# Fetching the transposed activations two tiles at a time, and a new place in the load queue for strip two's keys, values and last queries

## The chip, the cores and the metric

The kernel runs on one core of one Trainium2 chip. The metric is the device time of one execution in microseconds (us); lower is better. The kernel before was timed at 876.93 us, the median of three runs (875.13 to 880.14 us).

## What is computed

An attention block without softmax feeds a feed-forward block with squared ReLU. All values are float32. The inputs `q`, `k`, `v` have 8 batches, 8 heads, 576 positions and 64 features per head.

```python
kv  = einsum('bhsd,bhse->bhde', k, v)            # 64 x 64 per head
out = einsum('bhsd,bhde->bhse', q, kv)
rms = sqrt(mean(out * out, axis=-1, keepdims=True) + 1e-6)
x   = (out / rms * g_norm)                       # then (B,H,S,D) -> (4608 tokens, 512)
h   = x @ w_in                                   # 512 -> 2048
y   = (maximum(h, 0) ** 2) @ w_out               # 2048 -> 512
```

## The kernel before

**Tiles and strips.** The 4608 tokens are 36 tiles of 128 tokens, and 4 tiles make a strip of 512 tokens, so there are 9 strips, numbered s = 0 to 8 in the code. The change calls s = 2 "strip two" and s = 3 "strip three". For each strip the feed-forward block runs an up phase (x times `w_in`) and a down phase (times `w_out`). Both are cut by Strassen-like recombinations into sums and differences of blocks, so a strip has fewer products on TensorE (PE) and more additions on VectorE (DVE), ScalarE (ACT) and GpSimd (POOL). From strip 2 on (`DEEP_UP = 2`) both phases are recombined twice: the up phase has 55 steps (`up_slot`, L1248), the down phase 14 (`down_deep`, L1109), numbered 55 to 68. Nearly every up step is one group of 16 matmuls.

**Attention for later strips.** The attention part of a coming strip is spread between the steps of the present one. A list `slices` holds its pieces in order; `attend_between` (L778) decides per step which of them run, by planned costs on DVE and ACT. The pieces that matter here are `transposed_query` (L378: DVE transposes a loaded q tile), `key_value` (L415: K^T V on PE), `query` (L505: products of q with K^T V), `squares_x` (L641: DVE transposes 32x32 squares of a finished x tile into `x_q`) and `send_x` (L652: writes `x_q` to a scratch tensor `x_d` in DRAM). Tiles 9 to 35 take this way through DRAM.

**Reading x back.** `fetch_x` (L657) reads a tile from `x_d` into the strip's `xT` buffer with four transfers, one for each block of 32 partitions. It calls `open_xt` (L624), which takes a buffer for `xT` from the stream pool when the first tile of a strip is fetched. `xT` is the right-hand side of the up phase of that strip.

**Weights.** `stream` (L933) takes the next weight block into a buffer of the stream pool: `w_in_deep` blocks (768 KB) for the up phase, then for each of the seven down products one block from `w_out` (L945, 768 KB) and one from `w_deep` (L951, 1 MB). The pool has 6 buffers, one or two of them held by `xT`; an allocation takes the buffer that was freed longest ago, and its transfer waits until the last reader of that buffer is done. In the up phase `stream` runs at steps 10, 17, 24, 31, 38, 45 and 52, and once at step 5. The block taken at step 31 holds the first `w_out` block of the down phase, the one at step 38 the first `w_deep` block; PE reads them at steps 49, 51 and 53 of the up phase already (L1270) and again in the first down step. The block of step 45 is read from step 57 on, the one of step 52 in step 58.

**One queue for all transfers.** SyncE (SP) issues nearly all transfers, in program order: weights, outputs (L960), `x_d` writes, `xT` fetches, keys and values (L132, with `k_rest` and `v_rest` at L162), queries (L123, in half tiles of two transfers) and `q_rest` (L176). A transfer that has to wait holds up all behind it.

**Which step a load goes to.** `clock` counts planned microseconds: 1.2 for an up step from strip 2 on, 2.2 for an up step of strip 1, 3.2 for a down step. After each step at most one of three queues is served (L1401 to L1411): first `keys_due` (a key load falls due 2 us after the `key_value` that frees its buffer), then `tiles_due` (an x fetch falls due 6 us after its `send_x`, with longer times for tiles 9, 10 and 11), and only if neither was served `drip`, which takes one half of a q tile or one part of `q_rest`. Drips keep a least distance of 4.5 us in an up phase (2.1 us in strip 1, 3.3 us in a down phase) and stop in `quiet` steps, in strip 2 and later from step 37 to step 57.

Of the kernel before, what the change touches and what calls it, by code (L numbers as in the profile page):

```python
# [10 lines left out]
FP32 = mybir.dt.float32  # L11
# [9 lines left out]
def kernel(  # L21
# [34 lines left out]
    nc = tc.nc  # L56
    P = 128
# [4 lines left out]
    NP = H // 2  # L62
# [6 lines left out]
    NT = 4  # L69
# [2 lines left out]
    N_STRIP = N_TILE // NT  # L72
    DEEP = 1
    DEEP_UP = 2
    SQ = 32
    Q_ON_PE = 2
    BEHIND = 1.6
# [10 lines left out]
    dram = ctx.enter_context(tc.tile_pool(name="dram", bufs=1, space=bass.MemoryType.DRAM))  # L88
# [101 lines left out]
    drips, rest_drips, keys_due, tiles_due = deque(), deque(), deque(), deque()  # L190
    clock, dripped = [0.0], [0.0]

    def due(queue):
        if queue and queue[0][0] <= clock[0]:
            _, f, a = queue.popleft()
            f(*a)
            return True
# [376 lines left out]
    first = {}  # L574
# [49 lines left out]
    def open_xt(s):  # L624
        if s not in xt:
            if s == 0:
                xt[s] = xt_pool.tile([P, STRIP // SQ, NP, SQ], FP32, name="xT", tag="xT")
            else:
                t = stream_pool.tile([P, 4, FQ // 2, P], FP32, name="xT", tag="w_blk")
                xt[s] = t.rearrange("p n f e -> p (n f e)").rearrange("p (a q t) -> p a q t", q=NP, t=SQ)  # L630
        return xt[s]
# [18 lines left out]
    squared, sent = {}, {}  # L650

    def send_x(n):  # L652
        d = sent[n] = dram.tile([P, 4, NP, SQ], FP32, name="x_d", tag="x_d", bufs=2 * NT)
        nc.sync.dma_start(out=d, in_=squared.pop(n))
        tiles_due.append((clock[0] + {9: 30, 10: 36, 11: 24}.get(n, 6), fetch_x, (n,)))

    def fetch_x(n):  # L657
        s, i = divmod(n, NT)
        x, d = open_xt(s), sent.pop(n)
        for f in range(4):  # L660
            nc.sync.dma_start(
                out=x[ts(f, SQ), ts(i, 4)].rearrange("d a q t -> d a (q t)"),
                in_=d[:, f].rearrange("(a d) q t -> d a (q t)", a=4),
            )

    xc = {}
# [442 lines left out]
    def down_deep(s, k, i):  # L1109
# [3 lines left out]
        if s == N_STRIP - 1 and k == 6 and i == 1:  # L1113
# [19 lines left out]
            return  # L1133
        if k == 0 and s >= DEEP_UP:
            if i == 0:
# [202 lines left out]
    for s in range(N_STRIP):  # L1338
        attend(ready[s])
        if s == DEEP_UP - 1:  # L1340
            while queried:
                attend(slice_at[0] + 1)
            psums.close()
            fpsum = ctx.enter_context(tc.tile_pool(name="fpsum", bufs=5, space=bass.MemoryType.PSUM, reuse_waits="tile"))
            apsum = ctx.enter_context(tc.tile_pool(name="apsum", bufs=1, space=bass.MemoryType.PSUM, reuse_waits="tile"))
        if s >= DEEP_UP:
            steps = [(0.5, up_slot, (s, slot)) for slot in range(55)]
        elif s == 0:
            steps = [(2, up_first, (g, fh, i)) for g in range(NG) for fh in range(2) for i in range(2)]
        else:  # L1350
            steps = [(1, up, (s, g, p)) for g in range(NG) for p in ORDER]
        n_up = len(steps)
        if s < DEEP:

            steps += [(2, down, (s, p, i)) for p in (ORDER if s else (1, 2, 5, 6, 7, 3, 4)) for i in range(2)]
        else:
            steps += [(2, down_deep, (s, k, i)) for k in range(7) for i in range(2)]
        goal, begun = ready.get(s + 1, len(slices)), slice_at[0]
        if s >= DEEP_UP:
            goal = max(goal, min(ready[DEEP_UP] + (len(slices) - ready[DEEP_UP]) * (s - 1) // (N_STRIP - DEEP_UP - 1), len(slices)))  # L1360
            if s > DEEP_UP:
                goal = min(pair_ends, key=lambda end: abs(end - goal))
        total, done = sum(w for w, _, _ in steps), 0
        for i, (w, fn, a) in enumerate(steps):
            if s == 0 and i < n_up:

                if 4 <= i < 10:
                    convert(3 + i)
                if i == 0:
                    load_next()  # L1370
                    load_rest(1, nc.sync)
                    load_next()
                if i == 1:
                    load_next()
                if i == 2:
                    for b in range(2):
                        load_q_rest(b, nc.sync)
                if i == 14:
                    for b in range(2):
                        store_first(b)  # L1380
            elif s == 0 and i == n_up:
                convert(len(conversions))
                conv.close()

                stream_pool = ctx.enter_context(tc.tile_pool(name="stream", bufs=6, reuse_waits="tile"))
                sum_pool = ctx.enter_context(tc.tile_pool(name="sum", bufs=8, reuse_waits="tile"))
            if s == 0 and n_up <= i < n_up + 2:
                for g in range(2 * (i - n_up), 2 * (i - n_up) + 2):
                    sum_g1(0, g)
            if s == 0 and n_up + 2 <= i < n_up + 4:  # L1390
                for g in range(2 * (i - n_up) - 4, 2 * (i - n_up) - 2):
                    sum_g3(0, g)
            fn(*a)
            if s == 0 and i < 4:

                convert(3 + i)
            done += w
            if s:
                clock[0] += 3.2 if i >= n_up else 2.2 if s == DEEP else 1.2
                soon = tiles_due and tiles_due[0][2][0] // NT == s + 1  # L1400
                if i == n_up + 10:  # L1401
                    while tiles_due and tiles_due[0][2][0] // NT == s + 1:
                        _, f, a = tiles_due.popleft()
                        f(*a)
                elif not due(keys_due) and not (soon and due(tiles_due)):
                    least = 2.1 if s == DEEP else 4.5 if i < n_up else 3.3
                    quiet = n_up * 2 // 3 < i < n_up + 3 or s == DEEP and i > n_up + 9
                    quiet = quiet or s == DEEP and i < n_up and drips and drips[0][0] == load_q_rest
                    if not quiet and clock[0] >= dripped[0] + least:
                        dripped[0] = clock[0]  # L1410
                        drip(True)  # L1411
                if s == DEEP:
                    attend(begun + (goal - begun) * min(i + 1, 25) // 25)
                elif i < n_up:
                    attend_between(i, begun, goal, *(2, 34) if s == DEEP_UP else (0, 27), 38)
                if s == DEEP and i in (3, 4, 7, 9):
                    if i == 3:
                        last_sums = store_deep_sums(*deep_due.popleft())
                    next(last_sums, None)
                if s == DEEP and i == n_up - 3:  # L1420
                    leaf_sums(s, 4)
                if s == 1 and i in range(2, 23, 3):
                    deep_sums_in((1, 6, 5, 4, 0, 2, 3)[i // 3])
                if s == 1 and i in (17, 20, 21, 23):
                    stream()
                continue
            if i == n_up:
                nc.gpsimd.memset(open_xt(1)[:, 0, 0, 0:1], 0.0)
                stream(2)
            if i == n_up + 4:  # L1430
                stream()
            if i in (n_up + 8, n_up + 11):
                load(2, (i - n_up) // 11, nc.sync, "q")
            if i == n_up + 12:
                load_q_rest(2, nc.sync)
            if i - n_up in (7, 8, 9, 12):
                sums_in((7, 8, 9, 12).index(i - n_up))
            if i == n_up + 11:
                sums_x(1)
            n = i + 1 - (n_up - 6)  # L1440
            pairs, m = divmod(max(n - 2 * NP, 0), 3)
            attend(min(ready[0] + min(max(n, 0), 2 * NP) + (n >= 2 * NP) + 4 * pairs + (0, 2, 2)[m], goal))
            while deep_due and i not in (n_up + 1, n_up + 4, n_up + 12, n_up + 13):
                deque(store_deep_sums(*deep_due.popleft()), 0)
            if i == n_up + 2:
                store_first(2)
            if i == n_up + 3:
                for _ in range(2):
                    load_next(names="kv")
            if i == n_up + 6:  # L1450
                load_rest(2, nc.sync)
            if 11 <= i < n_up:

                convert((13, 13, 14, 15, 16)[i - 11])
# [30 lines left out]
```

## Time and profile before

| | before |
|---|---|
| time, median of 3 runs | 876.93 us (875.13 to 880.14) |
| the profiled execution | 876.18 us |
| its span, first to last instruction | 874.4 us |
| PE busy | 860.8 us (98%) |
| DVE busy | 722.9 us (83%) |
| ACT busy, POOL busy | 352.0 us (40%), 315.4 us (36%) |
| granted TensorE clock, mean | 1.000 |
| transfers on SP's queue | 82.5% of the 16 DMA engines' span, 234.33 MB |
| `xT` fetches | 108 of 64 KB |
| `x_d` writes | 27 of 256 KB |

The profile is of one execution. "Busy" is the time in which an engine works on an instruction; waiting for a semaphore and issuing a transfer do not count. The views that are used below: the page (shares, the chain of work that ended last, groups, DMA issues), the waits (who waited for whom: total us, times, longest), the timeline of one engine (start, duration, what, and in square brackets the idle time before it with what ended it) and the windows (busy time per engine in a stretch, granted clock, DMA share, GB/s). `SPq` is the queue of SP.

### The profile page before, as it was taken

The page shows a single profiled execution, that of the slowest core. Times are in us where ns is not written, and L with a number is a line of the kernel's source. Part 1 is how long each engine was busy: PE and PEld are TensorE (multiplying, and loading weights), DVE is VectorE, ACT ScalarE, POOL GpSimd, SP SyncE. Part 2 cuts the span into 40 slices and gives each one's busy share as a digit, 9 for nine tenths or more (in the row PEclk, how much of TensorE's full clock was granted, in tenths as well). Part 3 has the DMA queues.
Part 4 walks back from the last instruction along what each step waited for, and adds up shares of the span by engine and source line. Part 5 has one row for each costly group of instructions (what it writes and reads, how often), then busy time and mean ns, then how long its engine had stood idle before and what let it go on. Part 6 is the DMA issues. An engine that isn't in the chain of part 4 may idle for free.

```text
span 874.4 us, 32665 instructions
## 1 busy us (share of the span) xinstructions
PE 860.8 (98%) x14176; PEld 805.8 (92%) x14176; DVE 722.9 (83%) x1236; ACT 352.0 (40%) x805; POOL 315.4 (36%) x319
## 2 busy tenths in 40 slices
PE   8999999999999899999999999999999999999998
PEld 7445888889999899999999999999999999999998
DVE  3899998879867896889778977897889777975897
ACT  5799241320047402560358034811392147202710
POOL 1100004630458305650475045704471447144700
PEclk9999999999999999999999999999999999999999
DMA  9998998999988997989778978998668856885483
GB/s 306 328 311 251 285 372 237 283 339 346 305 219 205 338 328 242 239 290 338 245 213 261 344 268 228 271 346 287 189 238 293 295 173 218 299 283 196 175 313 120
DMA packets 170304, 236.49 MB, mean 270 GB/s; under 512 B 79536, under 2 KB 134576, under 8 KB 161840
## 3 DMA queue, kind: packets, MB, share of 16 engines
q1 hardware_dynamic: 169856, 234.33, 82.5%
q8 instruction: 111, 1.82, 0.8%
q14 instruction: 33, 0.27, 0.1%
q10 hardware_dynamic: 304, 0.07, 0.0%
HBM read 197.66 MB, written 36.70 MB: 268 GB/s over the span
## 4 chain that ended last, share of the span: by engine, by line
PE 82%; DVE 9%; DMA 4%; ACT 3%; issue 2%; SPq 1%; DVEq 0%; ACTq 0%
PE ps_A L842 35%; PE ps_B L842 30%; PE ps_C L842 5%; PE ps_A L847 4%; PE x_ps L468 2%; PE kv_ps L432 2%; PE ps_B L847 2%; DVE w_c L269 1%; DVE w_t L289 1%; DMA q<-in_q_dram 1%; DMA w_blk<-w_deep 1%; DMA w_deep<-w_t 1%; DVE wt L289 1%; DMA q_rest<-in_q_dram 1%; PE ps_C L847 1%
## 5 line engine op out<-in xcount | busy, mean ns | idle before, releaser
L842 PE MATMUL ps_B<-w_blk,g_s 128*64 128x128 f32 x2016 | 122.6, 273 | 0.0
L842 PEld LDWEIGHTS ps_B<-w_blk,g_s 128*64 128x64 f32 x2016 | 113.1, 137 | 0.1
L842 PE MATMUL ps_A<-x_l,w_in 128*64 128x128 f32 x1568 | 102.4, 273 | 0.6 <-ACT snap L1305 0.6
L289 POOL TENSOR_TENSOR x_l<-xT 128x256 f32<-128x256 f32 x21 | 15.9, 757 | 232.4 <-PE ps_A L842 184.3
L842 PE MATMUL ps_B<-w_blk,gt 128*64 128x128 f32 x1504 | 94.7, 273 | 2.8 <-DMA w_blk<-w_deep 1.6
L842 PE MATMUL ps_A<-w_blk,g_s 128*64 128x128 f32 x1536 | 92.7, 273 | 0.4 <-issue 0.4
L842 PEld LDWEIGHTS ps_A<-x_l,w_in 128*64 128x64 f32 x1568 | 88.9, 137 | 0.9 <-ACT snap L1305 0.8
L842 PEld LDWEIGHTS ps_B<-w_blk,gt 128*64 128x64 f32 x1504 | 85.1, 137 | 3.6 <-issue 2.2
L1300 POOL TENSOR_TENSOR snap<-snap,gt 128x512 f32<-128x512 f32 x35 | 46.2, 1319 | 113.1 <-ACT snap L1305 107.5
L842 PEld LDWEIGHTS ps_A<-w_blk,g_s 128*64 128x64 f32 x1536 | 86.1, 137 | 0.5 <-issue 0.5
L1305 ACT COPY snap<-ps_A 128x512 f32<-128x512 f32 x63 | 36.8, 585 | 105.0 <-PE ps_A L842 99.0
L1240 ACT ACTIVATE gt<-gt 128x512 f32<-128x512 f32 x112 | 70.1, 626 | 14.2 <-DVE gt L1300 14.2
L1241 ACT ACTIVATE gt<-gt 128x512 f32<-128x512 f32 x112 | 70.7, 631 | 3.6
L842 PE MATMUL ps_A<-w_blk,gt 128*64 128x128 f32 x1152 | 71.5, 273 | 0.0
L842 PEld LDWEIGHTS ps_A<-w_blk,gt 128*64 128x64 f32 x1152 | 65.0, 137 | 0.0
L1089 ACT COPY o_sb<-ps_A 128x128 f32<-128x128 f32 x24 | 6.4, 265 | 145.5 <-PE ps_A L842 110.2
L1088 DVE TENSOR_TENSOR o_sb<-o_sb,ps_B 128x256 f32<-128x256 f32 (+1 forms) x123 | 47.4, 386 | 15.8 <-ACT o_sb L1089 11.0
L289 DVE TENSOR_TENSOR gt<-gt 128x2048 f32<-128x2048 f32 (+1 forms) x29 | 59.7, 2063 | 0.0
L1300 POOL TENSOR_TENSOR gt<-gt,snap 128x512 f32<-128x512 f32 x42 | 52.6, 1282 | 17.7 <-DVE snap L1300 17.7
L842 PE MATMUL ps_B<-x_l,w_blk 128*64 128x128 f32 x784 | 51.3, 273 | 0.0
L842 PE MATMUL ps_A<-x_l,w_blk 128*64 128x128 f32 x784 | 51.2, 273 | 0.0
L1046 DVE TENSOR_TENSOR g_s<-gt 128x512 f32<-128x512 f32 x56 | 47.9, 856 | 0.0
(194 smaller groups left out, 1801.6 us busy)
## 6 DMA issues: line engine op xcount, KB each, us to landing
w_blk<-w_deep SPq DMA_DIRECT2D x56, 1024.0 KB, 7.2
w_blk<-w_out SPq DMA_DIRECT2D x56, 768.0 KB, 6.7
w_blk<-w_in_deep SPq DMA_DIRECT2D x49, 768.0 KB, 6.1
raw<-in_moe_w_in_dram SPq DMA_DIRECT2D x16, 512.0 KB, 7.0
raw<-in_moe_w_out_dram SPq DMA_DIRECT2D x16, 512.0 KB, 4.8
k<-in_k_dram SPq DMA_DIRECT2D x29, 256.0 KB, 4.8
v<-in_v_dram SPq DMA_DIRECT2D x29, 256.0 KB, 5.1
x_d<-x_q SPq DMA_DIRECT2D x27, 256.0 KB, 5.3
```

The lines of the kernel that those rows point to most:

```text
L269: yield nc.vector.scalar_tensor_tensor(out=ci, in0=high, scalar=-(2**30), in1=ci, op0=ALU.bitwise_and, op1=ALU.bitwise_or)
L289: eng.tensor_tensor(out=out, in0=a, in1=b, op=ALU.subtract)
L432: nc.tensor.matmul(ps[ts(h, D), i], lhsT=a, rhs=w, start=i == 0 and c == 0, stop=c == C, skip_group_check=True)
L468: nc.tensor.matmul(ps[half, r, i, ts(p, D)], lhsT=q[row, half], rhs=kvd[b, p][row, row], start=True, stop=True)
L842: nc.tensor.matmul(ps[half], lhsT=lhsT[:, half], rhs=rhs, start=start, stop=stop, skip_group_check=True)
L847: nc.tensor.matmul(bank[BANK[p]][:, i, :], lhsT=lhsT(k), rhs=rhs(k), start=p in (1, 5, 2) and i == 0 and k == 0, stop=k == n - 1, skip_gro ...
L1046: nc.vector.tensor_tensor(out=t, in0=a21, in1=a22, op=ALU.add)
L1088: add = lambda out, a, b: nc.vector.tensor_tensor(out=out, in0=a, in1=b, op=ALU.add)
L1240: nc.scalar.activation(o, o, AF.Relu)
L1241: nc.scalar.activation(o, o, AF.Square)
L1300: add = lambda eng, out, a, b: eng.tensor_tensor(out=out, in0=a, in1=b, op=ALU.add)
L1305: nc.scalar.copy(t, ps)
```

## The change

A constant `FIRST_SENT = 9` is new. The scratch tensor `x_d` now holds two tiles in one buffer (4 buffers in place of 8), each tile in its half. An even tile is only written; the fetch is put into `tiles_due` when the odd tile is written, and it reads both tiles with four transfers of 128 KB each. Tile 9, whose partner 8 does not go through DRAM, is fetched alone. The due times are those of the odd tile (30 us for 9, 24 us for 11, else 6 us).

The order of loads changes in two strips. In strip 2, key and value loads that fall due after steps 25 to 38 are held until step 39, and drips stop from step 24 on in place of step 37. In strip 3, the least distance between drips is 2.1 us in place of 4.5 us for the first 15 steps.

```diff
+    FIRST_SENT = 9
...
     def send_x(n):
-        d = sent[n] = dram.tile([P, 4, NP, SQ], FP32, name="x_d", tag="x_d", bufs=2 * NT)
-        nc.sync.dma_start(out=d, in_=squared.pop(n))
-        tiles_due.append((clock[0] + {9: 30, 10: 36, 11: 24}.get(n, 6), fetch_x, (n,)))
-
-    def fetch_x(n):
+        if n % 2 and n - 1 in sent:
+            d = sent.pop(n - 1)
+        else:
+            d = dram.tile([2, P, 4, NP, SQ], FP32, name="x_d", tag="x_d", bufs=NT)
+        sent[n] = d
+        nc.sync.dma_start(out=d[n % 2], in_=squared.pop(n))
+        if n % 2:
+            tiles_due.append((clock[0] + {9: 30, 11: 24}.get(n, 6), fetch_x, (n, 1 if n == FIRST_SENT else 2)))
+
+    def fetch_x(n, tiles):
         s, i = divmod(n, NT)
         x, d = open_xt(s), sent.pop(n)
+        first = i + 1 - tiles
         for f in range(4):
             nc.sync.dma_start(
-                out=x[ts(f, SQ), ts(i, 4)].rearrange("d a q t -> d a (q t)"),
-                in_=d[:, f].rearrange("(a d) q t -> d a (q t)", a=4),
+                out=x[ts(f, SQ), 4 * first : 4 * (i + 1)].rearrange("d a q t -> d a (q t)"),
+                in_=d[2 - tiles :, :, f].rearrange("n (a d) q t -> d (n a) (q t)", a=4),
             )
...
-                elif not due(keys_due) and not (soon and due(tiles_due)):
-                    least = 2.1 if s == DEEP else 4.5 if i < n_up else 3.3
-                    quiet = n_up * 2 // 3 < i < n_up + 3 or s == DEEP and i > n_up + 9
+                elif not (not (s == DEEP_UP and 24 < i < 39) and due(keys_due)) and not (soon and due(tiles_due)):
+                    least = 2.1 if s == DEEP or s == DEEP_UP + 1 and i < 15 else 4.5 if i < n_up else 3.3
+                    quiet = n_up * 2 // 3 < i < n_up + 3 or s == DEEP and i > n_up + 9 or s == DEEP_UP and i > 23
```

## The prediction

> **What bounds the kernel now.** The page comes first. PE is busy 98% of the span at a full granted clock, so a change that leaves PE's work alone can win only idle time of PE. Then PE's waits between 230 and 330 us (total, times, longest); from 330 on only 0.6 us for an ACT copy is listed.
>
> ```profile
> PE 860.8 (98%) x14176; PEld 805.8 (92%) x14176; DVE 722.9 (83%) x1236; ACT 352.0 (40%) x805; POOL 315.4 (36%) x319
> ```
> ```profile
> PE ps_B L842 <- DMA w_blk<-w_deep: 1.6, 1, 1.6
> PE x_ps L468 <- issue: 1.3, 1, 1.3
> PE ps_B L842 <- DMA w_blk<-w_out: 1.2, 1, 1.2
> PE ps_A L842 <- issue: 0.4, 1, 0.4
> PE ps_C L842 <- issue: 0.4, 1, 0.4
> PE x_ps L468 <- DVE qT_rest L388: 0.3, 1, 0.3
> ```
>
> All of it lies in strip 2: step 0 of its up phase starts at 236.5 us and the down phase at 295.4. Two waits are for weight blocks, one is for a transposed query, three have no releaser. PE's timeline shows where the weight waits stand: at steps 49 and 53, the first readers of the first two blocks of the down phase.
>
> ```profile
> 288.29 1.09 PE L842 MATMUL ps_B<-w_blk,gt 128*64 128x128 f32 x16 [1.17 <-DMA w_blk<-w_out]
> ...
> 293.64 1.09 PE L842 MATMUL ps_B<-w_blk,gt 128*64 128x128 f32 x16 [1.64 <-DMA w_blk<-w_deep]
> ```
>
> The question is why these blocks came late. Their buffers are freed by the products of steps 31 and 38, whose groups in PE's timeline end at 272.3 and 278.4. SP's timeline shows what it did instead:
>
> ```profile
> 271.08 0.96 SPq L123 DMA_DIRECT2D q<-in_q_dram  x2
> 272.08 0.49 SPq L132 DMA_DIRECT2D k<-in_k_dram  x1
> ...
> 274.15 1.98 SPq L162 DMA_DIRECT2D k_rest<-in_k_dram  x1
> 276.17 0.64 SPq L162 DMA_DIRECT2D v_rest<-in_v_dram  x1
> 277.44 2.40 SPq L661 DMA_DIRECT2D xT<-x_d  x4
> 281.09 1.61 SPq L123 DMA_DIRECT2D q<-in_q_dram  x2
> 282.80 0.43 SPq L945 DMA_DIRECT2D w_blk<-w_out  x1
> 283.33 0.92 SPq L123 DMA_DIRECT2D q<-in_q_dram  x2
> 284.34 0.44 SPq L654 DMA_DIRECT2D x_d<-x_q  x1
> 284.87 0.38 SPq L951 DMA_DIRECT2D w_blk<-w_deep  x1
> ```
>
> The block of step 31 goes out at 282.80, 10.5 us after its buffer is free; that of step 38 at 284.87, 6.5 us late, and the chain of waits gives it 8.63 us to land (293.5). Ahead of them stand 14 transfers for later tiles. They are slow because each waits for the landing of the one issued eight before it: in SP's waits from 268 to 284, fetches at L661 wait for q and v loads and queries at L123 for k and v loads, 3.5 us in all, with which those transfers have nothing to do.
>
> **The change, part by part.** I followed the queues by the code's clock (1.2 us an up step). Transfers of strip 2 by step (q4 2a is the first half of batch 4's queries for head pair 2, x12 is tile 12; outputs left out):
>
> ```
> step     before                          after
> 0-22     q3 3b, q4 0-1, x12 fetch         q4 0-2 (a half earlier each), no x fetch
> 23       x13 fetch (4 x 64 KB)            x12+x13 fetch (4 x 128 KB)
> 24       w_in, q4 2a                      w_in
> 25-29    6 key loads, x14 fetch, q4 2b    nothing
> 31       w_out                            w_out
> 33       q4 3a, x15 write                 x15 write
> 38       w_deep                           w_deep
> 39-42    x15 fetch                        6 key loads, x14+x15 fetch (4 x 128 KB)
> 45, 52   w_out, w_deep                    w_out, w_deep
> 58-66    q4 3b, 8 q_rest                  nothing; q4 3 and q_rest in steps 0-12 of strip 3
> ```
>
> *The first two blocks.* After step 24 only the write of x15 stands between the weights, and its transpose is long done (272.9 on DVE). So they go out when their buffers are free, about 272.3 and 278.4. The first lands after 6.7 us (median for `w_out` on the page), 279.0, and is due at 288.29 - 1.17 = 287.1. The second, at `w_deep`'s median of 7.2 us, lands at 285.6, at its longest of 10.2 us at 288.6; it is due at 293.64 - 1.64 - 1.17 = 290.8. Both waits go: **-2.81 us**.
>
> *Queries.* x10 (step 32 of strip 1) and x12 (step 10 of strip 2) are no longer fetched alone, and queries take their turns: q3 3b moves from step 0 of strip 2 into strip 1, q4 0b from step 11 to 4. DVE's waits for them (8.4 us in two, listed for L384) should go; PE feels the first as 0.26 us for `qT_rest`: **-0.26 us**. The lower bound is 0, if q3 3b still lands after 240.7.
>
> *The loads put behind.* Six key loads (1.3 MB) and the double x fetch (0.5 MB) now stand between step 38 and the blocks of steps 45 and 52. Issued from 278.8 in some 0.5 us each, the last key load leaves about 282 and lands 6.1 us later (median of L162), 288. The eight-back rule lets the x fetch and the third block out between 282 and 287; at 6.7 us the block lands by 293.7. It is due when ps_A begins in the chain, 299.11 - 2.81 = 296.3. The fourth leaves about 287.0 and lands by 294.2, at the longest by 297.2; it is due 48 products later, 298.9. I take 0, because all medians leave 2.6 us or more. The upper end is in the rivals. The keys themselves are used at step 2 of strip 3, near 335.
>
> *Strip 3.* Twelve more transfers in its first 13 steps. No PE wait stands in this strip before. Its tightest block is step 38's: issued at 378.04, landed 4.9 us later, due 384.54, so 1.6 us to spare. Between steps 24 and 38 SP now passes 15 transfers in place of 19, since x18 and x19 share four. Cost 0; if this cover were gone, every us of lateness over 1.6 would be paid.
>
> *Pairs elsewhere.* 4 + 13 x 4 = 56 fetches in place of 108: 52 x 0.43 us (median issue) = 22 us of SP's time, off PE's path, worth 0. The bytes stay. `xT` is taken later, so stream blocks between get a buffer that was freed earlier, never later. In strips 2 to 7 the last pair goes out by step 42, while the first reader is POOL at step 67; cost 0.
>
> Here a rule of the Trainium skill can be set against the row. In the trace the four 64 KB landings of one fetch lie 0.17 us apart, so they overlap. DMA: Bandwidth & Descriptors, section Anatomy of one DMA, gives about 2 us fixed per transfer; an estimate by it would be 52 x 2 = 104 us of transfer time saved, and if that were on the path the sum would be far lower.
>
> *Sum.* -2.81 - 0.26 = -3.07 us. The profiled execution took 876.18 us (span 874.4), 0.75 below the median of the three runs; -3.07 from the median gives **873.9 us**, faster by 0.35%.
>
> **Rivals.**
>
> *A, the forecast:* 873.9.
>
> *B, the wait moves behind.* The stretch with the late blocks moved 238 GB/s, the down phase 341 (windows; the last columns are granted clock, DMA share, GB/s):
>
> ```profile
> 272.00:293.50 21.50, 18.84 (x342) 18.38 (x338) 19.14 (x26) 18.64 (x39) 19.22 (x16) 1.00 0.90 238
> 293.50:334.00 40.50, 39.94 (x728) 39.84 (x730) 34.46 (x55) 4.11 (x10) 6.64 (x7) 1.00 0.96 341
> ```
>
> If the new bunch runs at 238 and starts when the second block lands (285.6): 1.83 MB take 7.7 us, the third block 3.3 (lands 296.6, 0.3 late), the fourth 4.4 (301.0, 1.8 late beyond that). 2.1 us come back: 876.0. At 341 nothing is late. Against it: the 238 include five 64 KB query loads in 128-byte rows, which the change takes out of this stretch.
>
> *C, more goes.* The waits without a releaser (1.34 + 0.39 + 0.41 us) are, I think, late instruction blocks: PE's 16 KB instruction packet at 261.4 to 262.5 is followed by the resumption at 263.85. They go if the transfers around them thin out: -2.14 more, 871.8. But earlier weights fill the same stretch, so I keep them. Runtime: NRT & Kernel Launch, section Instruction fetch mechanics, calls crossing a block "mostly hidden"; by it these waits would have another cause and stay.
>
> *D, slower.* One mechanism: the bunch behind the first blocks starts late and PE starves in steps 57 and 58. With the second block at its longest (288.6), at 238 GB/s the third lands at 299.6, 3.3 late, the fourth at 304.0, 1.8 more, and an instruction block queued in the same bunch costs what the one after the key loads of 249 to 254 cost, 1.34. Together 6.4: 876.93 - 3.07 + 6.4 = 880.3. It decides from the third block landing after 299.1. For it: the down phase already fills the DMA engines to 0.96, so nothing is caught up. Against it: it needs the worst row twice.
>
> *That the first blocks stay late* would need a wait still in front of them; x15's write is the only one left and has been ready for 5 us. At that the time stays 876.9. The two writes into one `x_d` buffer could be ordered one after the other; the four `w_deep` writes into one scratch tensor go out 0.4 to 1.2 us apart, long before they land, so I don't expect it.
>
> **Numbers.** A 0.52, B 0.20, C 0.13, D 0.10, first blocks still late 0.05. About 0.5% (4.4 us) is what a measurement here can tell from no change. Faster by more (under 872.5): most of C and a little of A, 0.16. Slower by more (over 881.3): the upper part of D, 0.07. Within: 0.77. The range goes from 871.0 (C and some scatter; the runs of before lie 1.8 below and 3.2 above their median) to 879.0; it leaves out most of D and the lower part of C.
>
> **What would show it.** Right: in strip 2 SP issues the blocks of steps 31 and 38 within 1 us of the ends of those steps' products, PE has no wait for `w_blk` at all, DVE none of several us for q, 56 `xT` fetches on the page. B or D: PE waits for `w_blk` at steps 57 and 58, just after the down phase begins. C: no gap without releaser near 262. Wrong altogether: new PE waits in strips 3 to 8, or fetches of two tiles that take more than twice as long to land.

## The result and the profile after

The changed kernel took 873.77 us (median of 11 runs, 870.78 to 875.30) beside 877.86 us for the kernel before in the same measurement (11 runs, 875.13 to 882.88). The ratio is 0.994, with a 95% interval of 0.992 to 0.996, so it is 3.5 to 7 us faster. A second measurement of both on another chip gave 870.94 us (6 runs) beside 878.38 us (23 runs), ratio 0.9925, interval 0.990 to 0.995. The forecast time, 873.9 us, was right; the forecast gain of 3.07 us (0.35%) lies under the lower end of both intervals (3.5 and 4.4 us).

The profiled execution of the changed kernel took 872.68 us, with a span of 870.8 us and a granted clock of 1.000; before it was 876.18 and 874.4. Line numbers are 1 higher than before ahead of the changed code and 5 to 7 higher from it on (L123 is now L124; L654 is L659, L661 is L668, L842 is L849, L945 is L952, L951 is L958). First the page's busy times, which answer to the first line shown of before:

```profile
PE 859.6 (99%) x14176; PEld 804.9 (92%) x14176; DVE 722.6 (83%) x1236; ACT 351.7 (40%) x805; POOL 315.3 (36%) x319
```

PE's work is the same. What changed is its idle time. The next line is all that PE waited for from 230 to 330 us, where before there were six lines and 5.2 us. Behind it stand two of the lines that PE's waits over the whole span still have:

```profile
PE ps_B L849 <- DVE snap L1307: 0.7, 1, 0.7
```
```profile
PE ps_B L849 <- DMA w_blk<-w_deep: 0.8, 1, 0.8
...
PE ps_B L849 <- issue: 0.5, 1, 0.5
```

Both waits for weight blocks in strip 2 are gone, and so are the three gaps without a releaser. In their place stand a wait for an addition on DVE (L1307) in strip 2 and, in strip 3, a wait for a weight block and a short gap without a releaser (near 354 us). PE's timeline has them at step 52 of strip 2 and at step 53 of strip 3:

```profile
287.67 1.09 PE L849 MATMUL ps_B<-x_t,w_blk 128*64 128x128 f32 x16 [0.73 <-DVE snap L1307]
...
380.22 1.09 PE L849 MATMUL ps_B<-w_blk,gt 128*64 128x128 f32 x16 [0.84 <-DMA w_blk<-w_deep]
```

SP's timeline of after shows the blocks of steps 31 and 38 of strip 2 at 269.52 and 275.63, where before had them at 282.80 and 284.87. The keys come behind them, and the next two blocks (283.03, 283.77) behind the double fetch:

```profile
269.52 0.34 SPq L952 DMA_DIRECT2D w_blk<-w_out  x1
270.86 0.32 SPq L659 DMA_DIRECT2D x_d<-x_q  x1
275.63 0.32 SPq L958 DMA_DIRECT2D w_blk<-w_deep  x1
276.00 0.43 SPq L133 DMA_DIRECT2D k<-in_k_dram  x1
...
279.77 3.16 SPq L668 DMA_DIRECT2D xT<-x_d  x4
283.03 0.40 SPq L952 DMA_DIRECT2D w_blk<-w_out  x1
283.77 0.34 SPq L958 DMA_DIRECT2D w_blk<-w_deep  x1
```

**Where the time went.** All kernels here run the same 14,176 matmuls in the same order, so the start of the same matmul can be compared from trace to trace. Before to after, the shift changes at these places (us):

| place | shift added |
|---|---|
| opening | -0.20 |
| `qT_rest`, strip 2 step 0 | -0.33 |
| gaps without releaser near 262, 270 and 316 | -1.61, -0.61, -0.70 |
| step 49 and step 53 of strip 2 (weight blocks) | -1.39, -1.78 |
| step 52 of strip 2 (new wait for DVE) | +0.88 |
| strip 3: near 354, step 53 | +0.41, +1.01 |
| strip 5 | +0.88 |
| all, to the last matmul | -3.40 |

So the sum of about -3 came out of other terms than forecast: 2.9 us more from gaps that the forecast kept, and 3.2 us given back in new waits. That the two nearly cancel is in good part luck. That calls for experiments.

### The profile page after: what moved, and what is told of

It reads as the page before. It is cut to its first block, busy times and chain, and to the rows that moved or that the text cites. A ratio compares the mean times of both kernels' runs of the same rounds, so it can differ in the third digit from the quotient of the medians.

```text
span 870.8 us, 32583 instructions
## 1 busy us (share of the span) xinstructions
PE 859.6 (99%) x14176; PEld 804.9 (92%) x14176; DVE 722.6 (83%) x1236; ACT 351.7 (40%) x805; POOL 315.3 (36%) x319
## 3 DMA queue, kind: packets, MB, share of 16 engines
q1 hardware_dynamic: 169024, 234.33, 82.9%
## 4 chain that ended last, share of the span: by engine, by line
PE 80%; DVE 10%; DMA 5%; ACT 2%; issue 2%; SPq 1%; DVEq 0%; ACTq 0%
PE ps_A L849 34%; PE ps_B L849 30%; PE ps_C L849 5%; PE ps_A L854 4%; PE ps_B L854 2%; DVE w_c L270 2%; PE kv_ps L433 2%; PE x_ps L469 2%; DVE w_t L290 1%; DMA w_deep<-w_t 1%; DVE wt L290 1%; DMA x_d<-x_q 1%; DMA xT<-x_d 1%; DMA w_blk<-w_deep 1%; PE ps_C L854 1%
## 5 line engine op out<-in xcount | busy, mean ns | idle before, releaser
L849 PE MATMUL ps_B<-w_blk,g_s 128*64 128x128 f32 x2016 | 122.0, 273 | 0.0
L849 PEld LDWEIGHTS ps_B<-w_blk,g_s 128*64 128x64 f32 x2016 | 112.6, 137 | 0.1
L849 PE MATMUL ps_A<-x_l,w_in 128*64 128x128 f32 x1568 | 102.6, 273 | 0.6 <-ACT snap L1312 0.6
L849 PE MATMUL ps_B<-w_blk,gt 128*64 128x128 f32 x1504 | 94.1, 273 | 0.8 <-DMA w_blk<-w_deep 0.8
L849 PE MATMUL ps_A<-w_blk,g_s 128*64 128x128 f32 x1536 | 92.2, 273 | 0.0
L849 PEld LDWEIGHTS ps_A<-x_l,w_in 128*64 128x64 f32 x1568 | 89.1, 137 | 0.9 <-ACT snap L1312 0.8
L1307 POOL TENSOR_TENSOR snap<-snap,gt 128x512 f32<-128x512 f32 x35 | 46.2, 1319 | 112.8 <-ACT snap L1312 108.7
L849 PEld LDWEIGHTS ps_B<-w_blk,gt 128*64 128x64 f32 x1504 | 84.6, 137 | 1.4 <-PE ps_B L849 1.0
L849 PEld LDWEIGHTS ps_A<-w_blk,g_s 128*64 128x64 f32 x1536 | 85.7, 137 | 0.0
L849 PE MATMUL ps_A<-w_blk,gt 128*64 128x128 f32 x1152 | 71.2, 273 | 0.0
L849 PEld LDWEIGHTS ps_A<-w_blk,gt 128*64 128x64 f32 x1152 | 64.7, 137 | 0.0
L1307 POOL TENSOR_TENSOR gt<-gt,snap 128x512 f32<-128x512 f32 x42 | 52.6, 1280 | 16.6 <-DVE snap L1307 16.6
L849 PE MATMUL ps_B<-x_l,w_blk 128*64 128x128 f32 x784 | 51.3, 273 | 0.0
L849 PE MATMUL ps_A<-x_l,w_blk 128*64 128x128 f32 x784 | 51.2, 273 | 0.0
```

The costliest lines, as they stand in the source:

```text
L849: nc.tensor.matmul(ps[half], lhsT=lhsT[:, half], rhs=rhs, start=start, stop=stop, skip_group_check=True)
L1307: add = lambda eng, out, a, b: eng.tensor_tensor(out=out, in0=a, in1=b, op=ALU.add)
```

## The experiments

Two theories. **H**: the order of loads carries the gain (keys held, queries moved), as the forecast has it. **P**: the pairs carry it, because SP's queue passes fewer transfers on its way to the weight blocks, and each transfer waits for the landing of the one issued eight before it.

### Each half of the change alone

*The pairs alone*: the kernel before with the paired fetch, and the old order.

```diff
-                elif not (not (s == DEEP_UP and 24 < i < 39) and due(keys_due)) and not (soon and due(tiles_due)):
-                    least = 2.1 if s == DEEP or s == DEEP_UP + 1 and i < 15 else 4.5 if i < n_up else 3.3
-                    quiet = n_up * 2 // 3 < i < n_up + 3 or s == DEEP and i > n_up + 9 or s == DEEP_UP and i > 23
+                elif not due(keys_due) and not (soon and due(tiles_due)):
+                    least = 2.1 if s == DEEP else 4.5 if i < n_up else 3.3
+                    quiet = n_up * 2 // 3 < i < n_up + 3 or s == DEEP and i > n_up + 9
```

> The kernel before with the paired fetch only; the order of keys, values and queries in strips two and three is left as it was. Theory H (the hold does it: the weight blocks of steps 31 and 38 of strip two are late because loads for later tiles stand ahead of them): six key loads and two query loads still stand ahead of the block of step 31, so PE still waits for at least one weight block at steps 49 to 53, 0.5 us or more, and the start of the down phase of strip two comes at most 3 us earlier than before (5.07 us earlier in the changed kernel). Theory P (the pairs do it: with four transfers in place of eight the queue is no longer held by the landing of the transfer eight before): no wait for a weight block in strip two, no wait for the transposed query, the gap of 1.34 us near 262 gone, the down phase starts 4 to 5 us earlier, time 3 to 5 us below before.

*The order alone*: the kernel before with those three lines as the change has them, and single fetches.

> The kernel before with the new order in strips two and three only (keys held in steps 25 to 38, no drips from step 24, faster drips in strip three); each tile fetched alone as before. Theory H: both waits for weight blocks in strip two gone, 3 us or more off the start of its down phase. Theory P: the blocks go out nearly on time too, but what came before step 24 stays: PE's 0.26 us for the transposed query, DVE's wait of about 5 us for a query near 259 and PE's gap of 1.3 us near 262; so at most 3.5 us of the 5.07 us are won.

Measured on one chip (kernel before: 878.72 us, 23 runs): the pairs alone 872.10 us, ratio 0.9919 (0.9896 to 0.9942); the order alone 878.53 us, ratio 0.9998 (0.9976 to 1.0021). The pairs are enough for the gain; the order without them gains nothing that can be measured. The down phase of strip 2 starts 3.2 us earlier than before with the pairs alone (292.18 us after 295.41) and 2.5 us earlier with the order alone (292.92). H had expected at most 3 with the pairs and 3 or more with the order, P 4 to 5 and at most 3.5; so H missed both by little, and P overrated the pairs in this strip. PE's waits from 230 to 400 us, first of the pairs alone, then of the order alone:

```profile
PE ps_B L849 <- DVE snap L1307: 0.7, 1, 0.7
PE ps_B L849 <- DMA w_blk<-w_deep: 0.7, 2, 0.5
```
```profile
PE ps_B L842 <- DMA w_blk<-w_deep: 2.8, 1, 2.8
PE x_ps L468 <- DVE qT_rest L388: 1.2, 1, 1.2
PE ps_B L842 <- DVE snap L1300: 1.0, 1, 1.0
```

With the pairs alone the blocks of strip 2 still go out late (278.34 and 281.86, behind keys and queries), but 4.5 and 3 us earlier than before, and that is nearly enough: 0.20 us of waiting is left at step 53, and the other 0.5 us of that line lie ahead of step 0, at 236.8 us. The order alone mends strip 2 as forecast, no wait for a weight block there, and gives it back in strip 3: the 2.8 us stand at step 53 of strip 3. SP's timelines show what stood ahead of that block, first in the order alone (379.00), then in after (373.13):

```profile
368.88 0.38 SPq L945 DMA_DIRECT2D w_blk<-w_out  x1
369.35 2.24 SPq L654 DMA_DIRECT2D x_d<-x_q  x1
371.64 1.09 SPq L123 DMA_DIRECT2D q<-in_q_dram  x2
372.83 1.86 SPq L661 DMA_DIRECT2D xT<-x_d  x4
375.23 0.85 SPq L123 DMA_DIRECT2D q<-in_q_dram  x2
376.12 2.78 SPq L661 DMA_DIRECT2D xT<-x_d  x4
379.00 0.38 SPq L951 DMA_DIRECT2D w_blk<-w_deep  x1
```
```profile
363.85 1.44 SPq L952 DMA_DIRECT2D w_blk<-w_out  x1
365.71 0.32 SPq L659 DMA_DIRECT2D x_d<-x_q  x1
366.08 2.64 SPq L124 DMA_DIRECT2D q<-in_q_dram  x4
371.06 1.96 SPq L668 DMA_DIRECT2D xT<-x_d  x4
373.13 0.39 SPq L958 DMA_DIRECT2D w_blk<-w_deep  x1
```

These rows alone account for little of the delay, since after has to wait from 368.72 to 370.99 for the write of `x_d` to land before its fetch. Most of it was there earlier: from the first output of strip 2 that SP issues behind 337 us, 53 transfers in 38.6 us lead to the block in the order alone, 43 in 35.3 us in after.

### The pairs in eight transfers, and the keys not held

*Eight transfers*: the change, with both tiles still fetched together, but by eight transfers of 64 KB.

```diff
-                out=x[ts(f, SQ), 4 * first : 4 * (i + 1)].rearrange("d a q t -> d a (q t)"),
-                in_=d[2 - tiles :, :, f].rearrange("n (a d) q t -> d (n a) (q t)", a=4),
+                    out=x[ts(f, SQ), ts(j, 4)].rearrange("d a q t -> d a (q t)"),
+                    in_=d[j % 2, :, f].rearrange("(a d) q t -> d a (q t)", a=4),
```

> The changed kernel, but a pair of tiles is fetched at the same place with eight transfers of 64 KB in place of four of 128 KB. Theory P (number of transfers): SP is held longer behind each pair; in strip three the block of step 38 goes out 1.5 us or more later, and PE's wait for it (0.84 us in the changed kernel) grows to 1.5 us or more; time 1 to 3 us above the changed kernel. Theory H (place in the order): within 1 us of the changed kernel, strip two unchanged.

*Keys free*: the change with its keys served when they fall due, ahead of the first blocks.

```diff
-                elif not (not (s == DEEP_UP and 24 < i < 39) and due(keys_due)) and not (soon and due(tiles_due)):
+                elif not due(keys_due) and not (soon and due(tiles_due)):
```

> The changed kernel without the hold: key and value loads go out in steps 25 to 27 of strip two again, ahead of the block of step 31; drips stay out of steps 24 to 54. Theory H: the block of step 31 goes out 3 us or more after its buffer is free; PE waits for weight blocks in strip two again, 0.5 to 1.5 us; time 0.5 to 1.5 us above the changed kernel. Theory P: no wait for weight blocks in strip two, time within 0.5 us of the changed kernel or below it, since nothing stands between steps 38 and 45 but the fetch.

On the same chip: eight transfers 875.30 us, ratio 0.9974 (0.9949 to 0.9999); keys free 871.04 us, ratio 0.9907 (0.9885 to 0.9929). Eight transfers keep strip 2 as in after (no block late) and lose in strip 3, where PE waits 2.3 us for the same block. SP spends 6.2 us on the eight. In after it is 1.96 us for the four, behind the 2.3 us of waiting for `x_d`; the block goes out 1.8 us sooner there, counted from the same matmul:

```profile
368.94 6.20 SPq L668 DMA_DIRECT2D xT<-x_d  x8
375.23 0.38 SPq L958 DMA_DIRECT2D w_blk<-w_deep  x1
```

So it is mainly the number of transfers, not the scratch layout or the later time of the fetch; a small share of these two is not excluded, since eight transfers (0.9974) came out a little ahead of the order alone (0.9998), with intervals that overlap.

The traces show how the number acts. No transfer on SP's queue starts before the one eight before it has landed, in any of the 14 profiles, while in each of them 72 to 122 start before the one seven before has landed. Nearly all transfers (661 of 664 in before) have the completion semaphore of the one eight before, so what is seen is a limit of eight semaphores taken in turn; whether the queue itself would take more wasn't tried. SP's waits that end with such a landing, added up from 185 to 760 us, are 25.0 to 30.0 us in the six profiles with single fetches on SP (both of before, the order alone, eight transfers with 29.1, and the hold alone and the late fetch, which follow below), and 13.3 to 17.9 us in the five of after, pairs alone and keys free. In the stretch of the first two blocks, 236 to 296 us, they are 6.9 and 4.6 us in before, 1.8 with the pairs alone and 0.3 and 1.3 in after.

And holding the keys, the edit on which the forecast put most of its sum, isn't needed once there are pairs.

### The same again, and the hold by itself

*Before again* and *after again* are the two kernels unchanged, for a second profile; *keys free, again* repeats the kernel above.

> The kernel before, unchanged, for a second profile. In the first one the largest single gap of strip 2 was 1.34 us without a releaser near 262 us (1.61 us from start to start), and it was absent in the profiles of the change, of the pairs alone, of the order alone, of the eight transfers and of the keys not held. Theory 'fixed': it belongs to the order of loads of the kernel before, so it stands here again at the same matmul with 1.2 to 1.8 us. Theory 'chance': it comes in some executions only, and here it is under 0.4 us. The two waits for weight blocks at steps 49 and 53 of strip 2 should stand again by both (1.2 and 1.6 us, each within 0.6). If the mean granted clock is 0.998 in place of 1.000, the windows should show one stretch of some 3.5 us at a half clock, behind a PE wait of over 2 us; at 1.000 none.

> The changed kernel, unchanged, as the control for the next two on the same chip. Near 873 us. If the wait of 0.84 us for w_deep at step 53 of strip 3 belongs to the kernel, it stands here again with 0.4 to 1.3 us; if it was one late landing (6.95 us, where others took 4.9 to 5.5), it is under 0.3.

> The changed kernel without holding the keys to step 39 of strip 2, run again beside the change on one chip. Theory P (the pairs carry the gain, the hold is not needed): not slower than the change, 0 to 2.5 us faster, no PE wait for a weight block over 0.5 us in strips 2 and 3. Theory H (the hold makes the blocks come on time): 1 to 3 us slower than the change, with waits for w_blk at steps 49 and 53 of strip 2.

*The hold alone*: the kernel before with one line of the change.

```diff
-                elif not due(keys_due) and not (soon and due(tiles_due)):
+                elif not (not (s == DEEP_UP and 24 < i < 39) and due(keys_due)) and not (soon and due(tiles_due)):
```

> The kernel before with one edit: the keys and values of strip 2 are held to step 39. Fetches stay single, queries keep their old pace, and the order of loads in strip 3 is that of before. Theory E (what strip 2 gains uses up the slack of strip 3, because there the transfers and not PE set when the block of step 38 is issued): the start of the down phase of strip 2 comes 2 to 5 us earlier than before, and at step 53 of strip 3 PE waits for w_deep by about that gain less 1.6 us, 0.8 to 3 us; the time ends 1 to 2.5 us under before. Rival F (it is the queries moved into strip 3 that crowd its queue): strip 3 has no such wait over 0.4 us, and all of the gain of strip 2 reaches the end.

Measured on one chip (before 878.38 us): after again 870.94 us, keys free again 872.24 us (870.63 to 878.12), the hold alone 877.59 us, ratio 0.9979 (0.9951 to 1.0007). The second profile of before has a span of 876.3 us. At the matmul that followed the gap of 1.34 us there is now nothing; the PE timelines around it, first profile and second:

```profile
261.76 0.75 PE L468 MATMUL x_ps<-kv_all,qT 64*64 64x64 f32 x34
263.85 0.68 PE L468 MATMUL x_ps<-kv_all,qT 64*64 64x64 f32 x28 [1.34 <-issue]
```
```profile
262.85 1.23 PE L468 MATMUL x_ps<-kv_all,qT 64*64 64x64 f32 x62
```

So this gap belonged to one execution, and "chance" was right. On its cause the traces say more than the prediction had: of the 15 gaps over 0.3 us without a releaser behind 130 us, in all 14 profiles, 14 end 1.3 to 1.7 us after the end of a 16 KB instruction packet (here 262.50 and 263.85). That fits the late instruction blocks of rival C; no run moved such a block to test it. Of the two waits for blocks in strip 2, the one at step 53 stands again (1.37 us), the one at step 49 is down to 0.31, and strip 3 has 0.57 at its step 53. In after again the 0.84 us of strip 3 are 0.18. The waits of this kernel wander by a microsecond from one execution to the next.

The hold alone shows rival B of the prediction, at the place that it named. The first blocks are on time, and PE waits in steps 57 and 58, for the blocks behind the bunch of keys and fetches:

```profile
295.40 1.97 PE L842 MATMUL ps_A<-w_blk,gt 128*64 128x128 f32 x32 [1.04 <-DMA w_blk<-w_out]
...
299.18 1.09 PE L842 MATMUL ps_A<-w_blk,gt 128*64 128x128 f32 x16 [0.94 <-DMA w_blk<-w_deep]
```

Step 53 of strip 3 has no wait (the block landed 0.17 us ahead of its reader), so rival F of the expectation was right on the wait and E failed: it takes the queries moved into strip 3 to crowd its queue. That all of the gain reaches the end, as F had it, can't be seen: the interval of the hold alone includes 1. Without the quiet steps, the keys cost in strip 2; with them, the queries cost in strip 3; the pairs make room in both.

### Fetches by another engine, and behind the block

*Fetch by GpSimd*: the kernel before, with `nc.gpsimd.dma_start` in place of `nc.sync.dma_start` in `fetch_x`.

> The kernel before with one edit: the xT fetches are issued by GpSimd in place of SP, still one tile at a time with four transfers of 64 KB. Bytes and number of transfers are those of before; SP has 108 issues less to pass. Theory P (the pairs gain because SP's queue, in which each transfer waits for the landing of the one eight before it, passes fewer transfers on the way to the weight blocks): the block of step 38 of strip 3 is issued by 375 us, where before took 378, PE waits less than 0.5 us for weight blocks in strips 2 and 3 and the time falls by 3 to 6 us, as with the pairs. Rival S (the gain is in the transfers themselves: 128 KB in one transfer lands sooner or leaves the DMA engines freer than 2 x 64 KB): nothing gained, 876 to 879 us, and the blocks come as late as before. Both allow a new cost: GpSimd issues in order, so its additions may stand behind a fetch that waits for its x_d to land; that would show as PE or DVE waits for POOL.

It took 900.62 us, ratio 1.021 (1.016 to 1.026), and settles nothing by its time: the allowed new cost swallowed all else. GpSimd waits in order for `x_d` and for its buffers, and DVE and PE wait for its additions. The waits of POOL and PE:

```profile
POOL xT L661 <- DMA x_d<-x_q: 27.0, 6, 16.7
...
POOL xT L661 <- PE ps_B L842: 15.5, 3, 6.4
...
PE ps_B L842 <- DVE snap L1300: 9.8, 3, 5.4
```

PE's list has no wait for a weight block at all, which fits P, but PE is so late that it proves little.

*Order, late fetch*: the order alone, with the eight fetches of tiles 18 and 19 behind the block of step 38 in strip 3.

```diff
-        tiles_due.append((clock[0] + {9: 30, 10: 36, 11: 24}.get(n, 6), fetch_x, (n,)))
+        tiles_due.append((clock[0] + {9: 30, 10: 36, 11: 24, 18: 13, 19: 13}.get(n, 6), fetch_x, (n,)))
```

> The order alone (single fetches, 878.5 us, PE wait of 2.8 us for w_deep at step 53 of strip 3), with one place changed: the eight 64 KB fetches of tiles 18 and 19 stand behind the block of step 38 of strip 3 on SP's queue, not ahead of it. Number and size of the transfers stay. Theory P (what costs is how many transfers SP passes ahead of that block, each of which waits for the landing of an earlier one): the block goes out at 372 to 375 us in place of 379, the wait at step 53 of strip 3 falls under 0.8 us, fewer runs show a granted clock under 1.000, and the time falls by 3 to 5 us, to 873 to 876: what the pairs give is had without pairs. Rival S (single fetches cost by themselves, wherever they stand; or the rest of strip 3 is late anyway): the wait moves to the blocks of steps 45 and 52, read from step 57 on, and the time stays within 1 us of the order alone, 877.5 to 879.5.

It took 876.18 us beside 878.84 for before, ratio 0.9971 (0.9946 to 0.9996): 2.7 us where P had expected 3 to 5. Two of its 12 runs have a mean granted clock under 1.000, of the order alone 9 of 12. SP's timeline:

```profile
371.96 2.45 SPq L123 DMA_DIRECT2D q<-in_q_dram  x4
374.51 1.87 SPq L951 DMA_DIRECT2D w_blk<-w_deep  x1
376.42 6.98 SPq L661 DMA_DIRECT2D xT<-x_d  x8
383.50 0.38 SPq L945 DMA_DIRECT2D w_blk<-w_out  x1
```

The issue of the block starts 4.5 us earlier than in the order alone, as P says, but takes 1.87 us in place of 0.38; counted from its start the block needs 8.57 us to land where it needed 4.92, and PE still waits 1.59 us, where P had expected under 0.8. The last of the eight fetches is issued at 383.10, when the block, eight issues before it, lands at 383.08: the rule that each transfer waits for the one eight before it, in one row. PE then waits 0.50 us for the block of step 52, behind them, as rival S had it. Place alone gives part of the gain; that the rest needs fewer transfers is argued from this, and the interval overlaps that of the order alone.

### The block of step 38 in strip 3, in all traces

All issue and landing times are from the start of the same matmul, some 25 us ahead of the reader (which follows it by 24.94 us where nothing waits). The spare time is 24.94 less the landing; where it is negative, PE waits for about that long.

| kernel | this matmul (us) | block issued | landed | spare |
|---|---|---|---|---|
| before; again | 359.60; 358.43 | +18.4; +19.4 | +23.4; +25.5 | 1.6; -0.6 |
| order alone | 356.19 | +22.8 | +27.7 | -2.8 |
| order, late fetch | 356.56 | +17.9 | +26.5 | -1.6 |
| hold alone | 356.39 | +19.5 | +24.7 | 0.2 |
| eight transfers | 354.53 | +20.7 | +27.3 | -2.3 |
| pairs alone | 355.48 | +18.2 | +23.7 | 1.3 |
| after; again | 354.27; 354.71 | +18.9; +19.0 | +25.8; +25.2 | -0.9; -0.2 |
| keys free; again | 353.99; 356.00 | +18.6; +18.5 | +24.0; +25.3 | 1.0; -0.4 |

PE comes to this place 1.9 to 5.6 us earlier than in the two profiles of before. With pairs the queue follows it (18.2 to 19.0, as in before); with the order alone it doesn't, and the gain of strip 2 is eaten. The spare 1.6 us of the prediction was that of one execution, and at PE's old time.

### A stall of known length

*Stall, short* and *stall, long*: the change, with one or three of the four transfers of tiles 18 and 19 issued again ahead of that block; the diff is of the short one, the long one has `(0, 1, 2, 3, 0, 1, 0)`. The repeated reads bring the same data.

```diff
-        for f in range(4):
+        for f in (0, 1, 2, 3, 0) if n == 19 else range(4):
```

> The changed kernel, with the first of the four transfers of tiles 18 and 19 issued once more behind them, ahead of the block of step 38 in strip 3: it waits for the first to land, so the block goes out 1 to 2 us later and PE waits at step 53 of strip 3 by 1 to 2.5 us in place of 0.2 to 0.8. Theory K (a stall of PE of over some 2 us lets the granted clock fall to a half for some 3.4 us, at 1.7 us more): where the stall is under 2 us the mean granted clock stays 1.000 and the time grows by the stall alone, 1 to 2 us over the change; where it is over 2 us some runs show 0.998 and are longer by another 1.5 to 2 us. Rival N (the clock has nothing to do with the stalls): clocks as in the change, 1.000 in all runs, whatever the stall.

> The same with three transfers issued again, each behind the landing of its forerunner: the block goes out 4 to 7 us later and PE waits 4 to 7 us at step 53 of strip 3. Theory K: every run shows a mean granted clock of 0.998 or less (one stretch of 3.4 us at a half is 0.5 x 3.4 / 870 = 0.002), the windows show the stretch right behind the stall, and the time grows by the stall and 1.7 us, 6 to 9 us over the change. Rival N: 1.000 in all runs and the time grows by the stall alone, 4 to 7 us.

These came from a remark on the order alone: behind its wait of 2.81 us the granted clock falls. Its windows (the last columns are clock, DMA share, GB/s):

```profile
380.00:384.00 4.00, 1.25 (x24) 1.01 (x20) 3.22 (x4) 2.49 (x5) 3.75 (x3) 1.00 0.95 338
384.00:388.00 4.00, 3.94 (x42) 3.97 (x44) 0.36 (x1) 0.55 (x1) 0.00 (x0) 0.57 1.02 413
```

The short stall missed its aim: in the profile the block landed 0.9 us before its reader, and the kernel took 872.57 us, as the change (10 runs, 3 of them with a mean clock under 1.000). The long one made a wait of 3.46 us, and the same fall of the clock:

```profile
383.67 1.98 PE L849 MATMUL ps_B<-w_blk,gt 128*64 128x128 f32 x16 [3.46 <-DMA w_blk<-w_deep]
385.40 1.88 PE L849 MATMUL ps_A<-x_l,w_in 128*64 128x128 f32 x16
```
```profile
380.00:384.00 4.00, 0.54 (x8) 0.36 (x6) 2.19 (x3) 2.52 (x4) 2.73 (x2) 0.96 0.97 398
384.00:388.00 4.00, 4.00 (x50) 4.00 (x48) 0.69 (x2) 0.00 (x0) 0.00 (x0) 0.62 1.00 414
```

Sixteen matmuls that took 1.04 us take 1.98. From 383.67 to 387.09, 3.42 us, PE falls back by another 1.68 us, on top of 3.62 for the stall itself. The kernel took 878.24 us, 5.7 over the short one, where 3.62 + 1.68 = 5.3 was to be expected. Nine of its ten runs had a mean clock under 1.000, of the 17 runs of the change none. Theory K holds in mechanism and size, though the wait was shorter than the 4 to 7 us that it was to be. The trace of the fetch by GpSimd agrees: it has five more slow stretches, one beside each of PE's five longest waits behind 130 us (2.77, 2.77, 2.82, 3.93 and 5.38 us), while the DMA share in 5 to 6 us around them goes from 0.14 to 0.78; so a burst of transfers isn't needed for it. That one run of the long stall stayed at 1.000 (877.57 us) leaves open at which length it sets in.

## Why the prediction was right, and where it was wrong

**Right.** What bounds the kernel; that both waits for weight blocks in strip 2 go and where the blocks then stand on SP's queue (269.5 and 275.6, forecast 272.3 and 278.4); that DVE's waits for q go, and the wait for `qT_rest` with them (-0.33, forecast -0.26); that neither end of rival D comes. The pairs are seen on the page as 52 fetches of 128 KB and 4 of 64 KB, as counted. Fetches of two tiles land in 4.8 us (median), those of one before in 4.1. The total of -3.07 us is near the -3.40 of the two profiles, but in good part by luck: the terms that it left out cancel.

**"The first two blocks: -2.81 us."** They gave 1.39 + 1.78 = 3.17 in that profile, more than the listed idle (1.17 + 1.64), since a wait is listed from the end of the last matmul: a group of 16 lasts 1.04 us, and the next one, where nothing waits, starts 0.17 us before that end. Then 0.88 came back at step 52, where PE now waits for an addition on DVE; its 0.72 to 0.74 us stand in nine of the twelve profiles of changed kernels. The step didn't ask what is late next between the two waits. And the second profile of before has only 0.31 + 1.37 there.

**"Pairs elsewhere ... worth 0."** This is the step that failed. The pairs alone gave the whole gain (ratio 0.9919), the order alone none (0.9998). The prediction had priced 52 issues at 0.43 us of SP's time and found SP off the path. But SP's queue in order, with each transfer held by the landing of the one eight before, sets when a weight block goes out: from 185 to 760 us the waits for such landings are 25.0 to 30.0 us with single fetches on SP and 13.3 to 17.9 with pairs. The forecast had named that rule for strip 2, and in strip 3 it had seen the pairs as cover (15 transfers in place of 19), but gave them no gain of their own. Its largest term went to the hold of the keys, which isn't needed once there are pairs.

**"Strip 3. Cost 0", with 1.6 us to spare.** With single fetches it costs 2.8 us (order alone). The spare time was read at PE's old times, and a gain in strip 2 uses it up. With pairs it was nearly right: 0.84 and 0.18 us. New waits of PE in strips 3 to 8 were the forecast's own sign of being wrong altogether; small ones came, in strips 3 and 5.

**"So I keep them"** (rival C's gaps). All three are gone from the profile of after, 2.92 us. But the largest is gone from the second profile of before too, so it was never a property of the kernel, while the one near 270 us stands there again, with 0.7 us. A gap of 1.2 us without a releaser stands in the second profile of keys free, near 354 us, at the same matmul as one of 0.5 us in after. That these gaps are late instruction blocks fits the packets' times and stays untried.

**Fixed costs of a transfer.** By the prediction's estimate from the Trainium skill's page DMA: Bandwidth & Descriptors, section Anatomy of one DMA, 52 transfers fewer would have saved 104 us of transfer time. That section's figure is for transfers that GpSimd issues, and these go out from SP. The queue's share of the DMA engines went from 82.5% to 82.9%, of 874.4 and 870.8 us: in the time that the packets took, nothing was saved.

```profile
q1 hardware_dynamic: 169024, 234.33, 82.9%
```

**The size.** In the two measurements of the change the gain is 4.1 and 7.4 us, more than 3. That the time was met to 0.1 us is partly luck: the forecast started from 876.93 us, and in the measurement of the change before came out at 877.86. Of 85 runs of before beside the experiments, 52 have a mean clock under 1.000; of the 17 runs of the changed kernel none has. Runs at exactly 1.000 average 876.80 us (33 runs of before) and 872.66 us (17 of the change), 4.1 apart. All 85 average 878.69, so 1.9 us of the distance go with the lower clock. No run with a profile of before fell under 1.000, so which of its waits let the clock fall wasn't seen.

**What stays open.** Which of hold and queries is worth keeping: after (873.77, 870.94), keys free (871.04, 872.24) and pairs alone (872.10) can't be told apart, and no variant here beats the change beyond doubt.

## What to carry to other kernels

Where one queue issues everything in order with a limited number of transfers in flight, count the transfers ahead of the urgent one and not only their bytes or the queue's busy time; merging small ones moves all that stands behind them. Spare time ahead of a load shrinks by whatever the stages before it gain, so work it out again at the new times. Read waits of a microsecond from two profiles of the same kernel before explaining them.

## What the runs showed of the hardware

- After PE had stood still for 2.81 us (order alone) and for 3.46 us (stall, long), the granted clock fell to a half for 3.4 us and PE lost a further 1.7 us each time; five waits of 2.77 to 5.38 us in the fetch by GpSimd had such a stretch too. After waits of 1.64 us (before) and 2.26 us (eight transfers) the profiled clock stayed at 1.00. TensorE: Matmul & The Clock Gate, section HAM oscillation, of the Trainium skill warns of idle gaps of over some 3.4 us; here 2.77 were enough.
- A wait costs 0.14 to 0.22 us more from start to start than the idle time listed for it (1.17 listed, 1.39 lost; 1.64 and 1.78; 3.46 and 3.62).
- A fetch on GpSimd's queue issues in 0.55 us, but GpSimd stood still for up to 16.7 us before one that had to wait for its data.
- After the end of a 16 KB instruction packet PE went on 1.3 to 1.7 us later in 14 of 15 gaps of over 0.3 us without a releaser.
